# A late load, four sums in banks of their own, and a rewoven first period in a one-core attention and mixing kernel

## The chip, the cores and the metric

The kernel runs on one core of one Trainium2 chip. The metric is device time in microseconds (us) from start to end of one execution. The profile's span, from the first to the last instruction, is about 2 us shorter than the device time of the same execution.

## The reference

Two parts follow each other for a batch of B = 8. The first is a cross attention in both directions, for H = 8 heads, between S = 512 rows of x and 32 rows of a state, with head size 64:

```python
scores = scale * x @ state.T ;  a  = softmax(scores) ;  xread = a  @ state     # 512 rows
scores2 = scale * state @ x.T ; a2 = softmax(scores2) ; sread = a2 @ x         # 32 rows
attn = concat([xread, sread], rows)            # (8, 8, 544, 64), heads then side by side: (8, 544, 512)
```

The second is a mixing layer on these 544 x 512 values per batch:

```python
X = fft(fft(x, axis=1), axis=2) ; mixed = real(X)
u = x + mixed
un = (u - mean(u)) / sqrt(var(u) + 1e-6)
out = u + relu(un @ w_ch1) @ w_ch2             # w_ch1 512 x 2048, w_ch2 2048 x 512
```

The kernel does the transforms as products with cosine and sine tables: first over the 544 rows ("first axis"), then over the 512 columns ("second axis"). Rows are folded with their mirror images beforehand, so that half the tables are enough.

## The kernel before

Every engine runs its instructions in the order in which the program lists them, so the order of calls is the schedule. Batch 0 goes through an opening of its own; from then on, periods follow in which the two layers of batch b, the transform of batch b+1 and the attention of batch b+2 are interleaved. The change touches the opening and the first period. The names: `turn` transposes on TensorE, `score`, `read`, `sread` and `state_rows` are the attention of batch 0, `fold` adds rows to mirror images, `terms_of` and `out_of` are the first axis of batch 0 (four sums j = 0 to 3, kept in PSUM, then copied to G), `over_d` is the second axis, `turn_u` transposes the centred rows, `warm(n)` is n TensorE products without use that only keep the engine busy.

The loads of x at the start; batch 1 follows batch 0 at once:

```python
    def load_x(b):
        xs = wk.tile([128, 4 * dm], F32, name="xs", tag="xs")
        ...
        if b == 0:
            for queue, n in ((nc.sync, 3), (nc.scalar, 6), (nc.scalar, 7), (nc.scalar, 2), (nc.sync, None), (nc.sync, 4), (nc.sync, 5),
                             (nc.scalar, 0), (nc.sync, 1)):      # None: the state of batch 0; 6 and 7 are single rows
                ...
    load_x(0)
    load_state(1, 2)
    load_x(1)
    turn_in_dram(2, 3)
    load_state(2, 3, s_dram)
    ...
    for lo, k0, c, t in (...):                  # 4 x tensor_scalar, arguments of the second table
        nc.gpsimd.tensor_scalar(gi[:, lo:lo + 128], ...)
    ...
    cast_x(0, lo=2, hi=3)                       # GpSimd: x to bf16, a quarter at a time
    more_constants()
    clears(0)
    for i in (1, 0):
        cast_x(0, lo=i, hi=i + 1)
    load_w1(0, 2)                               # from the GpSimd queue
```

The opening and the first axis of batch 0. The sums 0 and 1 lie in one tile of two banks, the sums 2 and 3 in tiles of the second set of PSUM pools, which can be had only when the opening's pool is closed:

```python
        def begin():
            two_ = x2("gp")
            acc.update({0: two_[:, 0], 1: two_[:, 1], 2: qt("gp"), 3: qt("gp")})
            for j in range(4):
                nc.tensor.matmul(acc[j][:, 0:NM], ..., start=True, stop=False)
    ...
    warm(12); turn_state(); warm(6); turn_x0(3); warm(3); turn_x0(2); turn_ends(); warm(3)
    score(3); warm(4); score(2); warm(4); turn_x0(1); read(3)
    ...; low(); load_w1(2, 4); more_loads()     # more_loads: state of batch 1, clears, cast_x(1), load of w2
    warm(3); turn_x0(0); read(2); second_table(); warm(4); score(1); warm(4); score(0); warm(4)
    read(1); warm(4); read(0)
    sin_table(); sine_c(); sine_s(); sread(); warm(8); state_rows(); sine_low(); second_sines()
    opening.close()                             # then the pools psX, psQ, psF
    warm(8); begin(); warm(8)
    fold(1)
    ...                                         # NC, NS: negated tables, on VectorE
    terms_of(0, 1), terms_of(1, 1); terms_of(0, "low"), terms_of(1, "low")
    fold(0)
    terms_of(2, 1), terms_of(3, 1)
    terms_of(0, 0); out_of(0); terms_of(1, 0); out_of(1)
    terms_of(2, "low"), terms_of(2, 0); out_of(2)
    terms_of(3, "low"), terms_of(3, 0)
    second_halves()                             # VectorE, 2 instructions
    out_of(3)
    keep_low(); exp_again(); over_d(0)
```

(Several calls stand on one line here; in the program each has its own.) The first period before: a list in fixed order. Q(i, r) is a sixteenth of layer 1 of batch 0 (16 products of 128 x 128), s1 and r1 are the attention of batch 1, t1 is the transform of batch 1, M[...] are quarter steps of layer 2 of batch 0 (4 products of 128 x 512):

```python
    for step in (
            add_sums(0, 1), centre_sums(0, 1), over_d(1), add_sums(0, 0), centre_sums(0, 0),
            warm(8), turn_u(0, 1), Q(0, 0), turn_u(0, 0), ..., copies1[2], last_loads, Q(1, 2), s1[0], Q(0, 3), s1[1], Q(1, 3), s1[2], Q(2, 0), s1[3],
            r1[0], Q(2, 1), r1[2], r1[1], Q(2, 2), r1[3], Q(2, 3), r1[4], r1[5], low_state, load_x3, Q(3, 0), r1[7],
            state_ones(2, B), spread x 4, done, first_roots, Q(3, 1), Q(3, 2)):
        step()
    weave((Q(3, 3), 0, 0.25), (t1, 0.2, 1), ([M[i] for i in (0, 4, 1, 5, 2, 6, 3, 7, 8, 9)], 0.33, 0.99), ..., (scores_next, 0.46, 1))
```

`weave` gives each stream a stretch between 0 and 1, spreads its steps evenly over the stretch, and emits all steps in the order of their positions. r1[7] ends with `fold` of batch 1 on VectorE (13 instructions), and t1 begins with the four products of the first axis (`over_s`), which read what fold leaves.

Of the kernel before, what the change touches and what calls it, by code (L numbers as in the profile page):

```python
# [12 lines left out]
F32 = mybir.dt.float32  # L13
# [17 lines left out]
def kernel(  # L31
# [73 lines left out]
    def load_state(lo, hi, src=state):  # L105
        nc.sync.dma_start(
            out=stf[:, lo:hi].rearrange("p b g d -> p (b g) d"),
            in_=src[lo:hi].rearrange("b (g hh) j d -> (hh j) (b g) d", hh=4),
        )
# [2 lines left out]
    xs_of = {}  # L112

    def load_x(b):
        xs = wk.tile([128, 4 * dm], F32, name="xs", tag="xs")
        xs_of[b] = xs
        v = xs.rearrange("p (i h d) -> p i h d", i=4, d=D)
        xb = x[b].rearrange("h s d -> s h d")
        parts = [
            (slice(0, 128), 0, xb[1:129]),  # L120
            (slice(0, 128), 1, xb[144:272]),
            (slice(0, 128), 2, xb[273:401]),
            (slice(32, 128), 3, xb[416:512]),
            (slice(0, 15), 3, xb[129:144]),
            (slice(16, 31), 3, xb[401:416]),
            (slice(15, 16), 3, xb[0:1]),
            (slice(31, 32), 3, xb[272:273]),
        ]
        if b == 0:
            for queue, n in ((nc.sync, 3), (nc.scalar, 6), (nc.scalar, 7), (nc.scalar, 2), (nc.sync, None), (nc.sync, 4), (nc.sync, 5),  # L130
                             (nc.scalar, 0), (nc.sync, 1)):
                if n is None:
                    load_state(0, 1)
                    continue
                ps, si, rows = parts[n]
                queue.dma_start(out=v[ps, si], in_=rows)  # L136
            return
        for ps, si, rows in parts:
            nc.sync.dma_start(out=v[ps, si], in_=rows)

    def cast_x(b, copy=nc.gpsimd.tensor_copy, lo=0, hi=4):
        copy(xin_bufs[b % 2][:, lo:hi, 1:513], xs_of[b].rearrange("p (i c) -> p i c", i=4)[:, lo:hi])  # L142

    load_x(0)
    load_state(1, 2)
    load_x(1)


    def turn_in_dram(lo, hi):
        nc.sync.dma_start(out=s_dram[lo:hi].rearrange("b h j d -> (b h) j d"),  # L150
                          in_=state[lo:hi, :, ::-1, :].rearrange("b h j d -> (b h) j d"))

    turn_in_dram(2, 3)
    load_state(2, 3, s_dram)

    for i in range(2):
        nc.vector.memset(xin_bufs[i][:, :, 0:514:513], 1.0)
# [53 lines left out]
    def absolute(q, f):  # L211
        nc.vector.tensor_scalar(q.bitcast(I32), in0=f.bitcast(I32), scalar1=0x7fffffff, scalar2=None, op0=ALU.bitwise_and)


    def turn(W, N, lf, cols, scratch):
        n = len(cols)
        f2d, q2d = scratch[:, 0:n * W], scratch[:, n * W:2 * n * W]
        f, q = [t.rearrange("p (n w) -> p n w", w=W) for t in (f2d, q2d)]
        def ends():
            for i, c in enumerate(cols):  # L220
                nc.vector.scalar_tensor_tensor(f[:, i, :], in0=lf, scalar=pf[:, c:c + 1], in1=q[:, i, :], op0=ALU.mult, op1=ALU.add)
            absolute(q2d, f2d)

        for i, c in enumerate(cols):
            nc.vector.tensor_scalar(q[:, i, :], in0=lf, scalar1=pn[:, c:c + 1], scalar2=float(1 << 23), op0=ALU.mult, op1=ALU.add)
        nc.vector.tensor_scalar(q2d, in0=q2d, scalar1=float(1 << 23), scalar2=-float(N), op0=ALU.subtract, op1=ALU.mult)
        return f, q, ends

    shrink = 1.0 - 1e-6
# [10 lines left out]
    f1, q1, turn_ends = turn(NM, Stot, lt, [0, 2], gen1)  # L240

    gi = gen2[:, 0:512].bitcast(I32)
    for lo, k0, c, t in ((0, 0, 3, 128.0), (128, 128, 3, 128.0), (256, 0, 4, 256.0), (384, 128, 5, pf[:, 6:7])):
        nc.gpsimd.tensor_scalar(gi[:, lo:lo + 128], in0=li[:, k0:k0 + 128], scalar1=pf[:, c:c + 1], scalar2=t,
                                op0=ALU.mult, op1=ALU.add)

    def second_table():
        nc.vector.tensor_scalar(gi, in0=gi, scalar1=dm - 1, scalar2=None, op0=ALU.bitwise_and)
        nc.vector.tensor_scalar(sgi, in0=pi_[:, 3:4], scalar1=1, scalar2=None, op0=ALU.bitwise_and)
# [36 lines left out]


    cast_x(0, lo=2, hi=3)
    more_constants()
    clears(0)  # L290
    for i in (1, 0):
        cast_x(0, lo=i, hi=i + 1)

    def load_w1(lo, hi):
        for q in range(lo, hi):
# [2 lines left out]
    load_w1(0, 2)  # L298

    def more_loads():  # L300
        state_blocks(1, 2, nc.gpsimd.tensor_copy)
        clears(1)
        nc.gpsimd.memset(stb[:, 2:].rearrange("p b g c -> p (b g c)").bitcast(F32), 0.0)
        cast_x(1)
        for q in range(4):
            nc.gpsimd.dma_start(out=w2[:, q * 4:(q + 1) * 4, :], in_=w2v[:, q * 4:(q + 1) * 4, :])

# [8 lines left out]
    def x2(name):  # L316
        return psX.tile([128, 2, 512], F32, name=name, tag="x")
# [362 lines left out]
    def transform(b):  # L680
# [10 lines left out]
        acc = {}  # L691

        def begin():
            two_ = x2("gp")
            acc.update({0: two_[:, 0], 1: two_[:, 1], 2: qt("gp"), 3: qt("gp")})
            for j in range(4):
                nc.tensor.matmul(acc[j][:, 0:NM], lhsT=XN[:, 0, :], rhs=xin_bufs[0][:, 0, 0:NM], start=True, stop=False)

# [86 lines left out]
        def centre_sums(k, r):  # L785
            t = ub[k, r] = wk.tile([128, 512], BF16, name="ub", tag="ub", bufs=5)
            ud = U[k][:, r, 0:512] if r == 0 else U[k][:, 1, 512:0:-1]
            if (k, r) == (1, 0):
                nc.vector.tensor_scalar(t, in0=ud, scalar1=-512.0, scalar2=S_of[k, r][:, 0:1], op0=ALU.mult, op1=ALU.add)
            else:  # L790
                nc.scalar.activation(t, ud, AF.Identity, bias=S_of[k, r][:, 0:1], scale=-512.0)
# [197 lines left out]

    turn_state, turn_x0, score, read, sread, state_rows, fold, low = open_batch()  # L990
    begin, terms_of, out_of, keep_low, over_d, add_sums, centre_sums, turn_u, spread, done = transform(0)
    warm(12)
    turn_state()
    warm(6)
    turn_x0(3)
    warm(3)
    turn_x0(2)
    turn_ends()
    warm(3)
    score(3)  # L1000
    warm(4)
    score(2)
    warm(4)
    turn_x0(1)
    read(3)
    nc.vector.tensor_copy(XTs[0], XRs[0][0:32, 0, :])
    low()
    load_w1(2, 4)
    more_loads()
    warm(3)  # L1010
    turn_x0(0)
    read(2)
    second_table()
    warm(4)
    score(1)
    warm(4)
    score(0)
    warm(4)
    read(1)
    warm(4)  # L1020
    read(0)
    sin_table()
    sine_c()
    sine_s()
    sread()
    warm(8)
    state_rows()
    sine_low()
    second_sines()
    opening.close()  # L1030
    psX = ctx.enter_context(tc.tile_pool(name="psX", bufs=1, space=bass.MemoryType.PSUM))
    psQ = ctx.enter_context(tc.tile_pool(name="psQ", bufs=3, space=bass.MemoryType.PSUM))
    psF = ctx.enter_context(tc.tile_pool(name="psF", bufs=3, space=bass.MemoryType.PSUM))
    pool_of = {"warm": (psF, "c")}
    warm(8)
    begin()
    warm(8)
    fold(1)
    for t, n in ((TC, NC), (TS, NS)):
        nc.vector.tensor_scalar(n, in0=t[:, 0, :], scalar1=-1.0, scalar2=None, op0=ALU.mult)  # L1040
    terms_of(0, 1), terms_of(1, 1)
    terms_of(0, "low"), terms_of(1, "low")
    fold(0)
    terms_of(2, 1), terms_of(3, 1)
    terms_of(0, 0)
    out_of(0)
    terms_of(1, 0)
    out_of(1)
    terms_of(2, "low"), terms_of(2, 0)
    out_of(2)  # L1050
    terms_of(3, "low"), terms_of(3, 0)
    second_halves()
    out_of(3)
    keep_low()
    exp_again()
    over_d(0)
    pool_of.pop("tile")
    s1, reads_next = attend(1)
    load_x3 = lambda: (load_state(3, B, s_dram), load_x(3))
    scores_next, reads_after = attend(2)  # L1060
    L, M, r1, t1 = layer1(0), layer2(0), reads_next, transform(1)
    W = lambda n: (lambda: warm(n))
    turns1, copies1, s1 = s1[0], s1[1:4], s1[4:]
    Q = lambda i, r: L[4 * r + i]
    low_state = lambda: (state_blocks(2, 3, nc.gpsimd.tensor_copy), cast_x(2), turned[2]())
    for step in (
            lambda: add_sums(0, 1), lambda: centre_sums(0, 1), lambda: over_d(1), lambda: add_sums(0, 0), lambda: centre_sums(0, 0),
            W(8), lambda: turn_u(0, 1), Q(0, 0), lambda: turn_u(0, 0),
            lambda: (add_sums(1, 1), centre_sums(1, 1)), Q(1, 0), Q(0, 1),
            lambda: turn_u(1, 1), lambda: (add_sums(1, 0), centre_sums(1, 0)), Q(1, 1), Q(0, 2), turns1, lambda: turn_u(1, 0),  # L1070
            copies1[0], copies1[1], copies1[2], last_loads, Q(1, 2), s1[0], Q(0, 3), s1[1], Q(1, 3), s1[2], Q(2, 0), s1[3],
            r1[0], Q(2, 1), r1[2], r1[1], Q(2, 2), r1[3], Q(2, 3), r1[4], r1[5], low_state, load_x3, Q(3, 0), r1[7],
            lambda: state_ones(2, B), lambda: [spread(k, r) for k, r in ((0, 1), (0, 0), (1, 1), (1, 0))], done,
            lambda: [r() for r in first_roots], Q(3, 1), Q(3, 2)):
        step()
    L = L[:11] + [Q(3, 3)]
    weave((L[11:], 0, 0.25), (t1, 0.2, 1), ([M[i] for i in (0, 4, 1, 5, 2, 6, 3, 7, 8, 9)], 0.33, 0.99),
          ([lambda: state_blocks(3, B, nc.gpsimd.tensor_copy)], 0.85, 0.85), (scores_next, 0.46, 1))
    l2 = M
    for b in range(1, B + 1):  # L1080
        reads_next = reads_after
# [47 lines left out]
```

## Time and profile before

| what | value |
|---|---|
| device time, median of 3 | 312.06 us (312.06 to 312.41) |
| span of the profiled execution | 309.9 us |
| TensorE matmul busy | 290.8 us, 94% |
| TensorE weight loads busy | 166.6 us, 54% |
| VectorE, ScalarE, GpSimd busy | 179.4, 136.7, 94.2 us |
| first product of layer 1 of batch 0 | at 28.05 us |
| first product of layer 1 of batch 1 | at 69.37 us |

In the profile PE is TensorE, PEld its weight loads, DVE VectorE, ACT ScalarE, POOL GpSimd and SP the engine that issues most transfers; ACTq and SPq are the queues of instructions that only start transfers. A line of the timeline gives the start in us, the busy time in us, engine, source line, operation, output<-inputs, shapes and how often, and in brackets the idle time of the engine before it and what ended it. A line of the list of waits gives who waited for whom, the total in us, how often, and the longest. A line of the table by stretches gives the stretch, its length, the busy time of PE, PEld, DVE, ACT and POOL with the count of instructions, the granted TensorE clock (1 is full), the busy share of the 16 transfer engines (over 1 where transfers overlap) and GB/s.

### The profile page before, as it was taken

The page shows a single profiled execution, that of the slowest core. Times are in us where ns is not written, and L with a number is a line of the kernel's source. Part 1 is how long each engine was busy: PE and PEld are TensorE (multiplying, and loading weights), DVE is VectorE, ACT ScalarE, POOL GpSimd, SP SyncE. Part 2 cuts the span into 40 slices and gives each one's busy share as a digit, 9 for nine tenths or more (in the row PEclk, how much of TensorE's full clock was granted, in tenths as well). Part 3 has the DMA queues.
Part 4 walks back from the last instruction along what each step waited for, and adds up shares of the span by engine and source line. Part 5 has one row for each costly group of instructions (what it writes and reads, how often), then busy time and mean ns, then how long its engine had stood idle before and what let it go on. Part 6 is the DMA issues. An engine that isn't in the chain of part 4 may idle for free.

```text
span 309.9 us, 6001 instructions
## 1 busy us (share of the span) xinstructions
PE 290.8 (94%) x2289; PEld 166.6 (54%) x2320; DVE 179.4 (58%) x442; ACT 136.7 (44%) x257; POOL 94.2 (30%) x213
## 2 busy tenths in 40 slices
PE   3977995999999999999999999999999999999996
PEld 3956884544644555556645454445554544555443
DVE  5665359968697666871826846684859383100112
ACT  4656774374662445235451455235533533333300
POOL 7695047466046022800316013600340041000000
PEclk9999999899999999999999999999999999999999
DMA  7999950594763674268542495244243014500345
GB/s 155 189 194 188 196 114 17 105 176 105 172 103 84 143 166 117 59 130 154 136 103 77 86 186 128 72 92 115 68 104 68 34 53 102 102 36 34 70 123 148
DMA packets 110906, 34.86 MB, mean 113 GB/s; under 512 B 102062, under 2 KB 106414, under 8 KB 110878
## 3 DMA queue, kind: packets, MB, share of 16 engines
q1 hardware_dynamic: 100126, 28.72, 43.6%
q0 software_dynamic: 4224, 4.19, 8.4%
q10 hardware_dynamic: 6528, 1.58, 2.3%
q8 instruction: 18, 0.29, 0.4%
q14 instruction: 10, 0.08, 0.1%
HBM read 22.41 MB, written 14.02 MB: 118 GB/s over the span
## 4 chain that ended last, share of the span: by engine, by line
PE 84%; DVE 7%; ACT 4%; issue 2%; ACTq 1%; POOL 0%; DVEq 0%
PE po L956 35%; PE ph L892 33%; PE gp L755 3%; PE ph L902 2%; PE warm L988 1%; PE yp L662 1%; PE po L948 1%; PE xrp L441 1%; PE xfp L441 1%; PE yp L661 1%; ACTq L136 1%; PE esp L416 1%; DVE U L666 1%; PE eTp L428 1%; PE srp L480 1%
## 5 line engine op out<-in xcount | busy, mean ns | idle before, releaser
L956 PE MATMUL po<-w,hT 128*128 128x512 bf16 x478 | 122.8, 382 | 1.6 <-issue 0.9
L894 ACT ACTIVATE hT<-ph 128x512 bf16<-128x512 f32 x112 | 66.8, 598 | 118.4 <-PE ph L892 116.3
L892 PE MATMUL ph<-unT,w 128*128 128x512 bf16 x435 | 112.7, 379 | 0.7
L892 PEld LDWEIGHTS <-w 128*128 128x128 bf16 x576 | 50.6, 98 | 47.4 <-issue 0.6
L956 PEld LDWEIGHTS <-hT 128*128 128x128 bf16 x496 | 47.3, 99 | 47.1 <-issue 1.1
L923 DVE SCALAR_TENSOR_TENSOR ot<-po,rstd,U 128x512 f32<-128x512 f32 (+2 forms) x33 | 24.2, 733 | 51.4 <-PE po L956 49.2
L759 POOL COPY GL<-G 128x128 bf16<-128x128 bf16 x7 | 2.0, 290 | 72.7 <-ACT G L756 72.7
L666 DVE TENSOR_TENSOR U<-yp,XR 128x512 f32<-128x512 f32 x14 | 9.6, 683 | 22.2 <-PE yp L662 22.2
L327 POOL TENSOR_TENSOR rstd<-mv,epst 128x1 f32<-128x1 f32 x34 | 7.2, 212 | 49.0 <-DVE mv L323 49.0
L321 DVE BATCH_NORM_STATS2 st<-U 128x6 f32<-128x512 f32 x32 | 21.7, 679 | 0.0
L328 POOL TENSOR_TENSOR rstd<-rstd,mhalf 128x1 f32<-128x1 f32 x34 | 20.0, 587 | 2.7
L756 ACT CAST G<-gp 128x288 bf16<-128x288 f32 x28 | 13.3, 485 | 10.8 <-PE gp L755 10.8
L902 PE MATMUL ph<-unT,w 128*128 128x128 bf16 x256 | 16.4, 219 | 0.9 <-ACT unT L822 0.9
L142 POOL CAST xin<-xs 128x2048 bf16<-128x2048 f32 (+1 forms) x10 | 15.5, 1555 | 2.3 <-DMA xs<-in_x_dram 2.2
L902 PEld LDWEIGHTS <-w 128*128 128x128 bf16 x256 | 15.0, 98 | 1.2 <-issue 1.0
L492 POOL COPY XT<-XR 32x514 bf16<-32x514 bf16 x7 | 4.2, 603 | 36.2 <-DVE XR L450 36.1
L988 PE MATMUL warm<-ident 128*128 128x128 bf16 x83 | 9.1, 258 | 4.2 <-POOL ident masks.py:199 3.5
L810 DVE TENSOR_SCALAR ub<-U,mv 128x512 bf16<-128x512 f32 x24 | 12.3, 511 | 0.9
L904 ACT ACTIVATE hT<-ph 128x512 bf16<-128x512 f32 x16 | 9.2, 596 | 3.3 <-PE ph L902 3.2
L450 DVE TENSOR_TENSOR XR<-xrp,rs 128x512 bf16<-128x512 f32 x14 | 9.7, 695 | 0.6
L450 DVE TENSOR_TENSOR XF<-xfp,rs 128x512 bf16<-128x512 f32 x14 | 9.7, 692 | 0.5
L666 DVE TENSOR_TENSOR U<-yp,XF 128x510 f32<-128x510 f32 x14 | 9.5, 677 | 0.0
(226 smaller groups left out, 375.8 us busy)
## 6 DMA issues: line engine op xcount, KB each, us to landing
xs<-in_x_dram SPq DMA_DIRECT2D x22, 256.0 KB, 5.4
w<-in_moe_w_ch_dram POOLq DMA_DIRECT2D x8, 512.0 KB, 8.6
out_dram<-ot SPq DMA_DIRECT2D x15, 256.0 KB, 3.8
r_dram<-ot SPq DMA_DIRECT2D x14, 256.0 KB
out_dram<-r_dram SPq DMA_DIRECT2D x14, 256.0 KB, 3.5
xs<-in_x_dram SPq DMA_DIRECT2D x8, 192.0 KB, 4.3
xs<-in_x_dram ACTq DMA_DIRECT2D x2, 256.0 KB
l_dram<-ot SPq DMA_DIRECT2D x2, 256.0 KB
```

The lines of the kernel that those rows point to most:

```text
L142: copy(xin_bufs[b % 2][:, lo:hi, 1:513], xs_of[b].rearrange("p (i c) -> p i c", i=4)[:, lo:hi])
L321: nc.vector.bn_stats(st6, u)
L328: nc.gpsimd.tensor_tensor(rstd, rstd, mhalf, op=ALU.pow)
L450: nc.vector.tensor_tensor(ov, in0=p[ps, :, 0:256].rearrange("p g (h d) -> p g h d", d=D), in1=rs[ps].unsqueeze(3).to_broadcast([n, 2, 4, D ...
L666: nc.vector.tensor_add(u.rearrange("p (k r) -> p k r", r=2), p.rearrange("p (r k) -> p k r", r=2)[:, 0:u.shape[1] // 2, :], x.rearrange("p ...
L756: nc.scalar.copy(G[:, j, :].rearrange("p (i q) -> p q i", q=2), p[:, 0:NM].rearrange("p (q i) -> p q i", q=2))
L810: nc.vector.tensor_scalar(t, in0=ud, scalar1=mv[:, 0:1], scalar2=None, op0=ALU.subtract)
L892: nc.tensor.matmul(ph[:, o:o + n], lhsT=w1[:, c, f * 128:(f + 1) * 128], rhs=un_of[key][:, c, :], start=(c == 0), stop=(c == DC - 1))
L894: nc.scalar.activation(hT[:, per * i:per * i + per, :].rearrange("p a b -> p (a b)"), ph, AF.Relu, scale=-1.0 / 512 if key == 0 else -1.0 ...
L902: nc.tensor.matmul(ph[:, o:o + 128], lhsT=w1[:, c, f * 128:(f + 1) * 128], rhs=un_of[key][:, c, 128 * r:128 * r + 128], start=(c == 0), st ...
L923: nc.vector.scalar_tensor_tensor(ot[:, cols], in0=po_of[i][:, 0:cols.stop - cols.start], scalar=rstd, in1=u[:, cols], op0=ALU.mult, op1=AL ...
L956: nc.tensor.matmul(po_of[i], lhsT=h_of[key][:, f, i * 128:(i + 1) * 128], rhs=w2[:, f, :], start=(f == 0), stop=(f == FC - 1))
```

## The change

It has three parts. The load of batch 1 no longer starts right after that of batch 0: a GpSimd memset into its buffer, placed behind the casts of batch 0, holds it back, and the loads of batch 0 are fewer and in another order. The four sums of the first axis get a bank each in the opening's own PSUM pool, so that they can be begun before the pool is closed. And the first period is woven by position, with layer 2 of batch 0 following layer 1 as filler for the transform of batch 1. Smaller moves go with it: other numbers of warm products, the table arithmetic on VectorE and GpSimd earlier or later, one centring on VectorE instead of ScalarE.

```diff
     def load_x(b):
+        row = v[15:32:16, 3]
...
-            (slice(15, 16), 3, xb[0:1]),
-            (slice(31, 32), 3, xb[272:273]),
+            (row, xb[0:273:272]),
...
-            for queue, n in ((nc.sync, 3), (nc.scalar, 6), (nc.scalar, 7), (nc.scalar, 2), (nc.sync, None), (nc.sync, 4), (nc.sync, 5),
-                             (nc.scalar, 0), (nc.sync, 1)):
+            for queue, n in ((nc.sync, None), (nc.scalar, 2), (nc.sync, 3), (nc.scalar, 0), (nc.sync, 4), (nc.sync, 5), (nc.sync, 6),
+                             (nc.sync, 1)):
...
     load_x(0)
-    load_state(1, 2)
-    load_x(1)
+    xs_of[1] = wk.tile([128, 4 * dm], F32, name="xs", tag="xs")
...
     cast_x(0, lo=2, hi=3)
+    for lo, k0, c, t in (...):                 # the 4 tensor_scalar, moved here
     more_constants()
-    clears(0)
     for i in (1, 0):
         cast_x(0, lo=i, hi=i + 1)
+    nc.gpsimd.memset(xs_of[1][0:1, 0:1], 0.0)
+    load_state(1, 2)
+    load_x(1)
+    turn_in_dram(2, 3)
+    load_state(2, 3, s_dram)
+    clears(0)
...
         def begin():
-            two_ = x2("gp")
-            acc.update({0: two_[:, 0], 1: two_[:, 1], 2: qt("gp"), 3: qt("gp")})
+            for j, tag in enumerate("ttee"):
+                acc[j] = ps0.tile([128, 512], F32, name="gp", tag=tag, bufs=2)
...
-            if (k, r) == (1, 0):               # centring on VectorE
+            if (k, r) in ((0, 0), (1, 0)):
...
+    warm(22); turn_state(); warm(8); turn_x0(3); turn_x0(2); turn_ends(); second_table(); warm(3)
+    score(3); score(2); read(3); turn_x0(1); ...; low(); load_w1(2, 4); state_blocks(1, 2)
+    read(2); turn_x0(0); warm(2); score(1); warm(2); score(0); warm(3); read(1); warm(3); read(0)
+    sin_table(); sine_c(); sine_s(); sread(); begin(); warm(10); state_rows(); sine_low(); second_sines(); warm(14)
+    fold(1); ...; terms_of(0, 1), terms_of(1, 1); terms_of(0, "low"), terms_of(1, "low"); fold(0)
+    second_halves(); more_loads()              # more_loads begins with cast_x(1)
+    terms_of(2, 1), terms_of(3, 1); terms_of(2, "low"), terms_of(3, "low")
+    terms_of(0, 0); out_of(0); terms_of(1, 0); out_of(1); terms_of(2, 0); out_of(2); terms_of(3, 0); out_of(3)
+    warm(8); opening.close()                   # then the pools psX, psQ, psF
+    over_d(0); exp_again(); add_sums(0, 1); centre_sums(0, 1); over_d(1); warm(12); turn_u(0, 1); add_sums(0, 0); centre_sums(0, 0)
+    Q(0, 0); last_loads(); turn_u(0, 0); ...; Q(1, 0); Q(0, 1); ...; Q(1, 1); turns1(); turn_u(1, 0); Q(0, 2); copies1
+    Ls = the other eleven Q, in the order (1,2) (0,3) (1,3) (2,0) (2,1) (2,2) (2,3) (3,0) (3,1) (3,2) (3,3)
+    weave((Ls + [M[i] for i in (0, 4, 1, 5, 2, 6, 3, 7, 8, 9)], 0, 1), (s1, 0.03, 0.18), (r1, 0.18, 0.45), (t1, 0.52, 0.95),
+          ([state_ones(2, B), spread x 4, first_roots, done], 0.44, 0.6), ([later_state], 0.5, 0.5), ([load_x3], 0.9, 0.9),
+          ([state_blocks(3, B)], 0.96, 0.96), (scores_next, 0.75, 1))
```

The lines with + from `warm(22)` on are abridged: several calls stand on one line.

## The prediction

> **What bounds the kernel now.** I read first the table by stretches, cut where the timeline shows stages to begin and end: ident ready, last scores, first term of the first axis, first product of layer 1, the r1[7] products, end of the fold, end of the slow clock, first layer 1 product of batch 1, end.
>
> ```profile
> core 0: us, PE busy (x) PEld busy (x) DVE busy (x) ACT busy (x) POOL busy (x), PEclk, DMA share, GB/s
> 12.00:19.70 7.70, 6.11 (x124) 5.34 (x123) 7.00 (x30) 6.71 (x11) 6.21 (x14) 1.00 1.13 173
> 19.70:28.05 8.35, 5.72 (x55) 3.68 (x53) 4.04 (x15) 4.20 (x8) 7.47 (x13) 1.00 1.14 195
> 28.05:46.10 18.05, 17.14 (x286) 16.20 (x286) 8.05 (x24) 12.41 (x25) 2.84 (x5) 1.00 0.97 163
> 46.10:53.00 6.90, 3.50 (x54) 3.11 (x54) 6.23 (x10) 3.55 (x7) 6.39 (x10) 1.00 0.04 10
> 53.00:58.60 5.60, 5.37 (x29) 3.19 (x31) 5.14 (x21) 1.45 (x3) 1.95 (x6) 0.70 0.40 78
> 69.40:309.90 240.50, 235.50 (x1596) 122.97 (x1621) 134.78 (x299) 95.70 (x180) 53.80 (x112) 1.00 0.46 102
> ```
>
> From 69.4 us on TensorE is busy 98% of the time (235.5 of 240.5), and the change doesn't touch that code: the gain must come before 69.4. There TensorE idles 2.6 us at 19.7 to 28.05 and 3.4 us at 46.1 to 53; at 53 to 58.6 it is busy, but at a granted clock of 0.70. Before 19.7 its busy time says little, as much of it is `warm`. So I went on to the timeline of the first 60 us, for what each stage waits for:
>
> ```profile
> 0.73 3.10 ACTq L136 DMA_DIRECT2D xs<-in_x_dram  x4
> 3.86 1.28 ACT L177 ACT_TABLE_LOAD   x1 [3.86 <-issue]
> 5.26 1.21 ACT L166 CAST stb<-gen 32x128 bf16<-32x128 f32 x4
> 9.08 1.60 POOL L142 CAST xin<-xs 128x512 bf16<-128x512 f32 x2 [1.18 <-DMA xs<-in_x_dram]
> ...
> 18.36 0.61 PE L988 MATMUL warm<-ident 128*128 128x128 bf16 x8 [0.73 <-ACT XR L634]
> ...
> 24.31 0.27 PE L661 MATMUL yp<-TEO,G 128*128 128x256 bf16 x1 [0.33 <-DVE TEO L271]
> ```
>
> ScalarE issues four loads until 3.83 and can only then load its table and cast the state, on which the first transposes wait. GpSimd waits 1.18 us for x of batch 0, while batch 1's load has been issuing since 4.70. At 18.36 the new pools wait for a copy out of the old one. At 24.31 the second axis waits for its table. Last, TensorE's waits from 20 to 80 us:
>
> ```profile
> PE gp L755 <- DVE XQ L517: 1.8, 1, 1.8
> PE gp L755 <- DVE XQ L518: 1.6, 1, 1.6
> PE ph L902 <- ACT unT L822: 0.9, 1, 0.9
> PE tp L819 <- ACT ub L791: 0.7, 1, 0.7
> PE gp L708 <- ACT G L738: 0.6, 1, 0.6
> ```
>
> The two longest are the fold of batch 1 on VectorE; the last is a term waiting for a copy of the other half of its tile.
>
> **What the Trainium skill says.** "TensorE: Matmul & The Clock Gate", Part 1: the array runs at half rate until it has been busy for a window of about 3.4 us, and goes back after an idle one. The trace agrees: a 128-column product starts every 0.11 us until about 12 us and every 0.055 after, and after the fold's two waits (1.8 and 1.6 us) the 512-column products take 0.43 us each instead of 0.22, until about 57 us. "DMA: Bandwidth & Descriptors", Queues, rings and completion order: each engine takes turns between the queues that have work. The trace fits: from 4.6 to 14 us both x batches move together at 205 GB/s. "SBUF — State Buffer", Who interferes with whom: a VectorE instruction with two SBUF inputs and a GpSimd one that reads SBUF exclude each other. In the fold the same addition takes 0.55 us (L517) and 2.11 us (L518), the second beside a GpSimd cast from 50.71 to 52.68.
>
> **Part 1, the opening.** ScalarE issues two loads instead of four. Its first took 1.27 us, a later one about 0.6 (from the chain of waits), so it is free at about 2.5 instead of 3.83, has its table at 3.8 and casts the state from 3.9 to 5.1 (before 5.26 to 6.47). TensorE is then bound by the 22 warm products: 3.46 + 22 x 0.11 = 5.8, against 6.53 for the last transposes of the state. Then come 8 warm ones (0.9), two transposes (0.43 each), 3 warm (0.3), one score (0.64), a second; the warm products between the scores are gone. That puts the first `read` at about 9.6, against 11.5; busy without a break from 3.46, TensorE may also reach full clock some microseconds before 12. The casts of batch 0's other rows follow GpSimd's 1.6 us of table arithmetic and 0.7 us of constants: at about 7.1 to 8.7 instead of 9.08 to 10.68, as their data no longer shares the engines. From there ScalarE sets the pace, with four exponentials and two copies of 0.6 us, and then the sine table, at about 12.8 instead of 14.78. VectorE's four reads (0.9 each) end at about 14.4 instead of 16.77. The heads' product, the tables and fold(1) follow, so the first term could come 2.0 earlier. A further 1.3 comes from `begin`, now before the heads' product: after it there is no pool to wait for (0.73), and 14 warm products stand there (about 0.8) instead of 1.9 us of warm, begin, warm at 18.36 to 19.7. Together 3.3: the first term at 16.4 instead of 19.7. Every step of this assumes data in time, and the order of loads is new (a quarter of x needs four transfers of one queue). I count 2.3.
>
> **Part 2, terms to layer 1** (19.7 to 28.05 before). One bank per sum: the 0.6 wait of L708 goes, and 0.2 to 0.3 of issue gaps with it. The second table's halves (0.85 + 0.53 on VectorE) come before the last terms rather than after: the last copy to G doesn't wait for them; it ran at 24.44, 0.46 after the last term. 0.5. The centring of (0,0) leaves ScalarE (0.72, at 27.02), so the copy of unT follows the transposes directly: 27.2 instead of 27.65. 0.45. The exponential's table load stays on ScalarE beside VectorE's add. Sum 1.75; I count 1.6. Layer 1 would begin 3.9 earlier, at about 24.1. w1's first half is issued at about the same time as before (10.6) and landed after 7.3 us in the median, so it is there.
>
> **Part 3, the first period.** Before r1[7] now stand 14 Q instead of 13, after it two instead of three. From r1[7] to the fold's first result pass 4.85 us (46.10 to 50.95), and two Q fill about 2: TensorE idles 2.4 to 2.7 there, 0.5 to 0.9 more than before. Against this, the second wait (1.6) gets M[0] (0.86) as filler. And with less idle in one stretch the clock may not fall: between 53 and 58.6 the 0.70 costs 5.6 x 0.3 = 1.7 us. I give it six chances in ten: 1.0. So -0.5, +0.9, +1.0: 1.4 gained. Something is given back: the bn_stats of batch 0 (four, 0.85 with aggregation, 3.4 us) stand on VectorE between the fold and the first add of batch 1, as before, so the chain fold, statistics, add, centre, transpose goes earlier only as the fold does, by about 3.4; only two M and a score of batch 2 lie between over_d(0) and the transpose that needs 3 us of VectorE and ScalarE. When TensorE is ahead by more, it waits there. 0.9 back.
>
> **Part 4, what the late load costs.** The transfer engines stand empty from about 7.5 to 9.6, some 2 us. They were full from 14 to 43 us, so the last x of batch 2 lands at about 45 instead of 43. Its cast was at 50.71 before; if all else is 4 us earlier, it is wanted at about 46. The w2 load lands before it; layer 2 wants it from about 47. Nothing lost, but nearly.
>
> **Sum:** 2.3 + 1.6 + 1.4 - 0.9 = 4.4 us. 312.06 - 4.4 = 307.6.
>
> **Rivals.** (a) The gain of the opening is eaten by data: the casts of batch 1 come after 22 us, w2 goes out later, and TensorE, 4 us earlier, waits for w2 or batch 2's x. For it: 29 us of full transfer engines and the hole in Part 4. Against it: SP's next load already waited for the cast of batch 1 at 24.1, and this cast comes no later if batch 1 lands by 20. It would leave 310 to 312. (b) The fold stays the bound of the first period: a longer single wait at the first over_s, the clock falls as before, and the new weave gains nothing, or loses 1 to 2 us behind the statistics. For it: one Q less behind r1[7]. Then 308.5 to 310. (c) All goes as worked out without discounts (opening 3.3, terms 1.75, clock kept 1.7 and M 0.9, no more than 0.5 back): a gain of about 6.5, 305.5. For it: every wait that the change goes for is there in the trace; against it: four serial chains (loads, ScalarE, GpSimd, VectorE) must all move by the same amount.
>
> **Range and chances.** Case (c) with some luck gives the lower end, 304.8; (a) the upper, 311.2. 2% is 6.2 us, below 305.8, which needs nearly all of (c): 0.20. Slower by 2% would need 6 us lost in 70: 0.03. Within 2%: 0.77.
>
> **What would show it right or wrong.** The table load of ScalarE at 2.5 instead of 3.86; the casts of batch 0 done by 9; the first term (L708 before) at 16.4 to 17.5; no wait of a term for a copy to G; the first Q near 24; one fold wait of 2.4 to 2.7 and a second under 1; granted clock 1.0 after it; the first layer 1 product of batch 1 near 65. The prediction is wrong if the casts of batch 0 still wait for data, if TensorE waits for w1, w2 or xin of batch 1 or 2, if the clock after the fold still falls, or if the time after 69.4 changes by over 0.5 us.

## The result, and the profile after

The change made the kernel slower: 321.37 us (319.74 to 322.82) against 312.06, a ratio of 1.029 with a 95% interval of 1.024 to 1.034. The prediction was 307.6 us with a range to 311.2.

The profiled execution has a span of 319.5 us. First the table by stretches of the kernel after, cut at the same events as before: first term of the first axis, first product of layer 1, the r1[7] products, the fold's first product, first product of the second axis of batch 1, and then the stretch round the start of layer 1 of batch 1 and the rest.

```profile
core 0: us, PE busy (x) PEld busy (x) DVE busy (x) ACT busy (x) POOL busy (x), PEclk, DMA share, GB/s
17.06:24.32 7.26, 6.02 (x64) 4.41 (x64) 5.07 (x21) 4.36 (x9) 1.27 (x4) 1.00 1.22 200
24.32:48.41 24.09, 19.66 (x303) 18.76 (x303) 8.04 (x24) 12.81 (x26) 10.62 (x17) 0.93 0.98 168
48.41:54.74 6.33, 2.17 (x37) 1.97 (x35) 5.67 (x9) 1.82 (x4) 5.60 (x9) 0.83 0.16 32
54.74:61.60 6.86, 6.86 (x35) 3.71 (x36) 5.58 (x22) 2.55 (x5) 2.81 (x8) 0.66 0.50 83
74.50:89.50 15.00, 11.96 (x94) 5.58 (x93) 8.72 (x22) 4.58 (x9) 8.28 (x13) 0.89 0.67 122
89.50:319.50 230.00, 226.98 (x1537) 117.78 (x1533) 126.00 (x278) 90.98 (x173) 48.50 (x102) 1.00 0.47 102
```

The opening did what it was meant to do: layer 1 begins at 24.32 instead of 28.05. In the next row TensorE idles 4.4 us (24.09 less 19.66) where before it idled 0.9, then 4.2 us round the fold (before 3.4), then it is busy at a clock of 0.66 (before 0.70), and near 80 us it idles 3.0 us more. The waits of TensorE from 20 to 100 us name them (who waited for whom, total us, how often, longest):

```profile
PE gp L756 <- DVE XQ L518: 4.2, 1, 4.2
PE ph L893 <- ACT hT L895: 3.0, 1, 3.0
PE xTp L389 <- POOL xin L141: 2.9, 1, 2.9
PE eTp L406 <- ACT xT L395: 1.2, 1, 1.2
PE xrp L442 <- ACT ET L430: 1.1, 1, 1.1
```

The distance between the two kernels, taken at five events of both timelines (us), shows where each part of the loss falls:

| event | before | after | after less before | change since the row above |
|---|---|---|---|---|
| first product of layer 1, batch 0 | 28.05 | 24.32 | -3.7 | -3.7 |
| r1[7], last read of batch 1's attention | 46.10 | 48.41 | +2.3 | +6.0 |
| first product after the fold of batch 1 | 50.98 | 54.74 | +3.8 | +1.5 |
| first product of layer 1, batch 1 | 69.37 | 74.52 | +5.2 | +1.4 |
| product of layer 1 behind the first scores after it | 79.64 | 89.53 | +9.9 | +4.7 |

From the last row to the end both need the same: 309.9 - 79.64 = 230.3 and 319.5 - 89.53 = 230.0 us. So 13.6 us are lost between 24 and 90 us, and nothing behind. The timeline of the kernel after gives the story of each loss (start, busy us, engine, line, operation, output<-inputs, and in brackets the idle time and its releaser):

```profile
9.43 9.95 SPq L138 DMA_DIRECT2D xs<-in_x_dram  x7
9.86 1.72 POOL L298 DMA_DIRECT2D w<-in_moe_w_ch_dram  x2
15.41 1.54 POOL L298 DMA_DIRECT2D w<-in_moe_w_ch_dram  x2
29.77 2.00 POOL L141 CAST xin<-xs 128x2048 bf16<-128x2048 f32 x1 [11.31 <-DMA xs<-in_x_dram]
31.82 1.69 PE L389 MATMUL xTp<-ident,xin 128*128 128x128 bf16 x16 [2.90 <-POOL xin L141]
...
51.93 2.27 POOL L141 CAST xin<-xs 128x2048 bf16<-128x2048 f32 x1
52.36 1.86 DVE L517 COPY XE<-SS 128x2 f32<-128x2 f32 x1
54.74 0.30 PE L756 MATMUL gp<-TC,XQ 128*128 128x144 bf16 x1 [4.17 <-DVE XQ L518]
...
68.35 0.37 SPq L938 DMA_DIRECT2D r_dram<-ot  x1
72.35 0.42 SPq L106 DMA_DIRECT2D gen<-s_dram  x1
76.46 2.98 POOL L161 CAST stb<-gen 32x640 bf16<-32x640 f32 x4 [6.36 <-DMA gen<-s_dram]
79.48 1.09 ACT L895 ACTIVATE hT<-ph 128x512 bf16<-128x512 f32 x2 [6.57 <-POOL stb L161]
80.13 1.86 PE L893 MATMUL ph<-unT,w 128*128 128x512 bf16 x4 [3.04 <-ACT hT L895]
```

The instructions of the same loads, casts and copy in the kernel before:

```profile
4.70 8.46 SPq L139 DMA_DIRECT2D xs<-in_x_dram  x8
10.62 1.72 POOL L296 DMA_DIRECT2D w<-in_moe_w_ch_dram  x2
22.22 1.89 POOL L142 CAST xin<-xs 128x2048 bf16<-128x2048 f32 x1
...
50.09 0.26 DVE L516 COPY XE<-SS 128x2 f32<-128x2 f32 x1
59.49 0.59 SPq L106 DMA_DIRECT2D gen<-s_dram  x1
```

Three groups. **x of batch 1:** its held load is issued from 9.43 on, but 0.4 us later the load of w1 starts beside it, and GpSimd waits 11.3 us for the data; TensorE's transposes stand behind its cast. **The fold:** a copy of two elements per partition takes 1.86 us on VectorE instead of 0.26, and ends when GpSimd's cast of batch 2 does (54.22 and 54.20). **Batch 3:** its load now stands in SP's queue behind the first stores (68.35) and is issued at 72.35, instead of 59.49 before. The cast of its state waits 6.4 us for it at the head of GpSimd's queue, ScalarE then waits for GpSimd and TensorE for ScalarE.

### The profile page after: what moved, and what is told of

The parts are those of the page before. It is cut to its first block, busy times and chain, and to the rows that moved or that the text cites. A ratio compares the mean times of both kernels' runs of the same rounds, so it can differ in the third digit from the quotient of the medians.

```text
span 319.5 us, 6034 instructions
## 1 busy us (share of the span) xinstructions
PE 296.2 (93%) x2324; PEld 168.0 (53%) x2324; DVE 179.7 (56%) x443; ACT 135.6 (42%) x256; POOL 94.8 (30%) x214
## 4 chain that ended last, share of the span: by engine, by line
PE 79%; DMA 7%; DVE 5%; POOL 4%; ACT 1%; SPq 1%; issue 1%; POOLq 0%; DVEq 0%
PE po L957 35%; PE ph L893 32%; DMA xs<-in_x_dram 5%; PE gp L756 3%; PE ph L903 2%; DMA gen<-s_dram 1%; POOL xin L141 1%; PE po L949 1%; PE yp L663 1%; PE yp L662 1%; PE xrp L442 1%; POOL stb L161 1%; PE esp L417 1%; DVE U L667 1%; SPq L138 1%
## 5 line engine op out<-in xcount | busy, mean ns | idle before, releaser
L957 PE MATMUL po<-w,hT 128*128 128x512 bf16 x496 | 126.9, 385 | 0.0
L893 PE MATMUL ph<-unT,w 128*128 128x512 bf16 x448 | 114.7, 381 | 3.0 <-ACT hT L895 3.0
L893 PEld LDWEIGHTS <-w 128*128 128x128 bf16 x576 | 50.8, 98 | 50.6 <-issue 4.0
L141 POOL CAST xin<-xs 128x2048 bf16<-128x2048 f32 (+1 forms) x10 | 15.8, 1587 | 12.4 <-DMA xs<-in_x_dram 11.3
L903 PEld LDWEIGHTS <-w 128*128 128x128 bf16 x256 | 15.7, 101 | 1.3 <-issue 1.1
L989 PE MATMUL warm<-ident 128*128 128x128 bf16 x87 | 8.2, 252 | 3.5 <-POOL ident masks.py:199 3.5
L488 DVE TENSOR_TENSOR XR<-srp,rcs 32x128 bf16<-32x128 f32 x24 | 6.9, 287 | 5.9 <-POOL XT L493 4.4
## 6 DMA issues: line engine op xcount, KB each, us to landing
w<-in_moe_w_ch_dram POOLq DMA_DIRECT2D x8, 512.0 KB, 10.9
```

The lines of the kernel that those rows point to most:

```text
L893: nc.tensor.matmul(ph[:, o:o + n], lhsT=w1[:, c, f * 128:(f + 1) * 128], rhs=un_of[key][:, c, :], start=(c == 0), stop=(c == DC - 1))
L903: nc.tensor.matmul(ph[:, o:o + 128], lhsT=w1[:, c, f * 128:(f + 1) * 128], rhs=un_of[key][:, c, 128 * r:128 * r + 128], start=(c == 0), st ...
L957: nc.tensor.matmul(po_of[i], lhsT=h_of[key][:, f, i * 128:(i + 1) * 128], rhs=w2[:, f, :], start=(f == 0), stop=(f == FC - 1))
```

## The experiments

Theory A says that two separate waits for data cost the most: x of batch 1 is late because w1 is loaded beside it (about 4.5 us), and batch 3's load is late in the weave (about 4.7 us). Theory B says that these are one cause, the late batch 1. Theory C takes the weave itself, with too little filler at the fold, for the loss. Theory L came up on the way: GpSimd's casts keep VectorE out. (The expectation of e6 calls this "the lock".) Every kernel ran beside the kernel before, whose median there was 312.0 to 312.3 us; ratios are to those runs.

**e1: the load of batch 1 no longer held** (the rest of the change as it is).

```diff
     load_x(0)
-    xs_of[1] = wk.tile(...)
+    load_state(1, 2); load_x(1); turn_in_dram(2, 3); load_state(2, 3, s_dram)
...
-    nc.gpsimd.memset(xs_of[1][0:1, 0:1], 0.0)
-    load_state(1, 2); load_x(1); turn_in_dram(2, 3); load_state(2, 3, s_dram)
```

> The changed kernel with the load of batch 1 issued right behind that of batch 0, as before; all else as changed. Theory A (two separate data waits: batch 1's x lands late because it shares the transfer engines with w1, cost about 4.5 us; batch 3's load stands late in the weave, cost about 4.7 us): the wait for x of batch 1 at 29.77 goes, the cast of batch 1 ends before 24, the late load of batch 3 stays; 316 to 317.5 us. Theory B (one cause: everything after follows from the late batch 1): 311 to 312.5. Theory C (the new weave with its fold gap is the loss, data waits only fill the gap): over 319.

Measured: 320.86 us, 1.027 (1.022 to 1.033). Only C's number fits (over 319), and not for C's reason. The wait for x of batch 1 is gone, but nothing is gained: layer 1 begins at 28.09 instead of 24.32. The timeline of e1 shows why:

```profile
19.47 1.89 POOL L141 CAST xin<-xs 128x2048 bf16<-128x2048 f32 x1
19.49 3.94 DVE L270 TENSOR_SCALAR TEO<-TEO,sg 128x512 bf16<-128x512 bf16 x1
24.58 0.27 PE L662 MATMUL yp<-TEO,G 128*128 128x256 bf16 x1 [2.66 <-DVE G L739]
```

With the data early, GpSimd's cast and five memsets behind it fill 19.47 to 23.3 us. The second table's half, 0.34 us on VectorE in the kernel after, lasts 3.94 us beside them, and the second axis waits 2.7 us for the copy to G that comes after; the clock is 0.66 from 25 to 30 us. A wait of 2.9 us was traded for one of 2.7. This led to theory L.

**e2: batch 3's load earlier in the weave; e3: e1 and e2 together.**

```diff
-([load_x3], 0.9, 0.9)
+([load_x3], 0.5, 0.5)
```

> The changed kernel with the load of batch 3 moved from position 0.9 to 0.5 of the first period, behind the cast and transposes of batch 2; all else as changed. Theory A: its issue moves from 72.4 to about 61, GpSimd's wait of 6.4 us for the state goes, and with it TensorE's 3.0 us and the slow clock behind it; 316 to 317.5 us. Theory B: the load is late only because batch 1 was; it stays a wait; 320 to 321.5. Theory C: no more than 1 us gained.

> Both edits, batch 1's load early and batch 3's load at 0.5. Theory A: the gains add, 310.5 to 312.5 us, because the wait at the fold (4.2 us) and the slow clock after it are left. Theory B: like the first edit alone. Theory C: over 316.

Measured: e2 316.32 us, 1.011 (1.008 to 1.014); e3 315.91 us, 1.011 (1.006 to 1.016). e2 is as A expected: the load is issued at 60.96, the wait of 3.0 us near 80 is gone, and 5.1 us come back although batch 1 is as late as before. So B falls: batch 3 is a loss of its own. e3 fits none of the three (A expected 310.5 to 312.5): that the early load of batch 1 adds nothing agrees with e1. Three of e2's 15 runs, the profiled one among them, were in a slower state; without them its median is 316.1, which moves each difference taken with it below by 0.2.

**e4: w1 behind the held load of batch 1** (both halves of w1 where its second half was); **e5: e4 and e2 together.**

```diff
     cast_x(0, lo=i, hi=i + 1)
-    load_w1(0, 2)
...
     low()
-    load_w1(2, 4)
+    load_w1(0, 4)
```

> The changed kernel with batch 1's load held as it is, but the first half of w1 issued with the second (about 15 us instead of 9.9), so that batch 1's x has the transfer engines alone until then. Theory A (the sharing with w1 made it late, not the hold alone): batch 1's cast begins before 22 instead of 29.77, the first layer 1 products may wait for w1 by up to 2 us; 316.5 to 319 us. Rival (the hold and the slow issue of the load make it late whatever else moves): the cast begins after 26, and the time stays at 320 or more.

> The changed kernel with the first half of w1 issued with the second, and the load of batch 3 at 0.5. Theory A (two separate data waits, each now removed by an edit that worked alone: about 5 us each): 310 to 312 us. Rival (one wait takes the place of the other, as when the early load of batch 1 gained nothing): 314 to 316.

Measured: e4 315.61 us (315.13 to 319.18), 1.014 (1.007 to 1.021), better than expected; e5 311.17 us, 0.998 (0.996 to 1.000), as A expected. The timeline of e4:

```profile
9.61 5.07 SPq L138 DMA_DIRECT2D xs<-in_x_dram  x7
15.48 3.20 POOL L298 DMA_DIRECT2D w<-in_moe_w_ch_dram  x4
20.08 1.89 POOL L141 CAST xin<-xs 128x2048 bf16<-128x2048 f32 x1
```

With w1 out of the way the same seven transfers take 5.07 us to issue instead of 9.95, and batch 1 is cast at 20.08 instead of 29.77, without any other change: w1's bytes made it late. The two gains add, 5.8 and 4.4 us (e4's four runs scatter by 4 us, so tenths don't count here).

The fold's longest wait fell too, from 4.2 to 2.5 us, which was not expected. The timeline of e5 at the fold:

```profile
48.48 0.16 DVE L515 COPY XE<-SS 128x2 f32<-128x2 f32 x1
48.68 0.43 DVE L516 TENSOR_TENSOR XQ<-XE 128x256 bf16<-128x256 f32 x1
49.00 2.19 POOL L141 CAST xin<-xs 128x2048 bf16<-128x2048 f32 x1 [1.01 <-DMA xs<-in_x_dram]
49.35 1.86 DVE L518 CAST XN<-XE 128x2 bf16<-128x2 f32 x1
```

(The fold's lines have numbers lower by two here: the copy is L515.) The copy that took 1.86 us takes 0.16 here. Batch 2's load is being issued until 47.44 us here (38.32 in the kernel after), GpSimd waits 1.01 us for it, and its cast then meets a VectorE instruction *behind* the fold's first result instead of one ahead of it.

**e6: e5 with batch 2's casts on ScalarE.**

```diff
-    later_state = lambda: (state_blocks(2, 3, nc.gpsimd.tensor_copy), cast_x(2), turned[2]())
+    later_state = lambda: (state_blocks(2, 3), cast_x(2, nc.scalar.copy), turned[2]())
```

> The same, with the state and the x of batch 2 cast by ScalarE instead of GpSimd. Theory L (GpSimd's casts keep VectorE out while it folds: a 2-element copy took 1.86 us beside the cast): no fold instruction above 0.9 us, TensorE's fold waits together 1.5 us shorter or more, the time 1 to 2.5 us lower than without this edit. Rival (the fold's own chain and the two Q behind it make the wait, the lock is hidden): within 0.7 us of it, or slower as ScalarE delays its copies.

Measured: 310.22 us, 0.994 (0.993 to 0.996), 0.95 less than e5, just under what L expected. No VectorE instruction of the fold takes over 0.8 us any more, and in the profiled execution the clock stays at 1.00 from 40 to 60 us (e5: 0.76 from 50 to 55). That execution, at 309.1 us, is one of 7 in 20 whose mean clock was 0.999 or more; e5 has 7 such too. The medians of these differ by 1.8 us, those of the other 13 by 0.8, so the gain isn't the clock's alone. L holds for the VectorE instructions, but its 1.5 us at TensorE's fold waits didn't come: the first wait is 2.4 us after 2.5, the fold's own length behind r1[7].

**e7: e3 with GpSimd's cast of batch 1 held** until the second table is made, by a one-element copy that reads it.

```diff
     def more_loads():
+        nc.gpsimd.tensor_copy(gate[:, 3:4], TEO[:, 3, 1, 127:128])
         cast_x(1)
```

> Batch 1's load early and batch 3's load at 0.5, as in the third run, and in addition GpSimd's burst of casts, clears and memsets held until VectorE has done the second table's halves (by a one-element copy that reads them). Theory L (this burst kept VectorE out: the half took 3.94 us against 0.35, and the second axis waited 2.7): the half takes under 0.5 us, TensorE's wait of 2.7 goes, 311 to 313 us. Rival (VectorE is late there for another reason): no change, 315 to 316.

Measured: 312.91 us, 1.002 (1.000 to 1.004), as L expected. The table's half takes 0.34 us, the wait of 2.7 us is gone, and 3.0 us with it. This is e1's loss made and unmade by GpSimd's place alone.

**e8: new opening and sums, w1 behind batch 1, but the first period in the old order; e12: the same with w1 at its place**, so the change with its weave left out.

```diff
-    Ls = ...; weave((Ls + [M[i] ...], 0, 1), (s1, 0.03, 0.18), (r1, 0.18, 0.45), (t1, 0.52, 0.95), ...)
+    for step in (keep_low, Q(0, 0), turn_u(0, 0), ...): step()      # the list of the kernel before from there on
+    weave((Q(3, 3), 0, 0.25), (t1, 0.2, 1), ([M[i] ...], 0.33, 0.99), ..., (scores_next, 0.46, 1))
```

> The new opening and sums with w1 behind batch 1's x, and the first period in the order of the kernel before (batch 3's load is early in it). Theory A with the weave as a loss of its own: it has three Q behind the fold's products and the opening is 3.5 us earlier, so 308 to 309.5 us, below the fifth run. Rival (the weave is worth something once its loads are in time): 311 or more, above the fifth run.

> The changed kernel with its opening and sums as they are (load of batch 1 held, w1 at its place), but the first period in the old order: the weave is left out. It is the kernel with the old period and w1 behind the load of batch 1, at 308.4 us, with w1 moved back. Theory A (the shared engines cost the same whatever the period): 3.5 to 5.5 us more, 312 to 314, with the cast of batch 1 waiting until about 29.8 us, TensorE waiting 2 to 4 us for it near 30 to 34 us, and the x of batch 2 cast 4 us later or more than at 48.8. Rival: the old period takes the late batch 1 better, as its transposes come later and its other work fills the wait: less than 2 us more, under 310.4.

Measured: e8 308.37 us, 0.989 (0.985 to 0.993), as expected. e12 310.45 us, 0.995 (0.993 to 0.996): faster than before, and 2.1 us above e8, where A expected 3.5 to 5.5 and the rival under 2. So A's size for the late batch 1 holds only inside the weave; C, that the weave itself costs, has a large share. The waits of e12:

```profile
PE gp L756 <- DVE XQ L518: 1.8, 1, 1.8
PE gp L756 <- DVE XQ L519: 1.6, 1, 1.6
PE xTp L389 <- POOL xin L141: 1.5, 1, 1.5
```

Batch 1 is cast at 29.70, as late as in the kernel after, but the wait for it is 1.5 us instead of 2.9 (the clock falls behind it here too, to 0.53 from 34 to 36 us). The waits of 1.2 and 1.1 us in batch 1's attention are not there, and the fold has the two waits of the kernel before. e8 has a new wait instead (a line of its waits: the scores of batch 2 for a transpose of x):

```profile
PE esp L415 <- DMA xT<-xin: 2.6, 2, 1.7
```

**e9: e8 with the scores of batch 2 later in the weave.**

```diff
-(scores_next, 0.46, 1))
+(scores_next, 0.66, 1))
```

> The eighth run (new opening, w1 behind batch 1's x, old order of the first period) with the scores of batch 2 spread over 0.66 to 1 instead of 0.46 to 1. If its wait of 2.6 us for the transposed x of batch 2, with the slow clock after it, is what is left of the late load there, 2 to 3 us less than the eighth run: 305.5 to 306.8. Rival (VectorE's statistics of batch 0, between fold and add, hold that stretch anyway): within 1 us of it.

Measured: 307.74 us (306.61 to 310.05), 0.987 (0.983 to 0.991). That wait is gone, but only 0.6 us of median came of it, and the intervals of e8 and e9 overlap. Three of e9's six runs took 306.6 to 306.8 us, less than any of e8's, and three 308.7 to 310.1; what separates them is not shown. It has the lowest median of the study, and is faster than both kernels.

**e10: the kernel before with the sums in banks of their own**, begun before the heads' product, with the order of terms and the earlier table halves that go with it; no hold, no weave.

```diff
-            two_ = x2("gp")
-            acc.update({0: two_[:, 0], 1: two_[:, 1], 2: qt("gp"), 3: qt("gp")})
+            for j, tag in enumerate("ttee"):
+                acc[j] = ps0.tile([128, 512], F32, name="gp", tag=tag, bufs=2)
```

> The kernel before with only the sums changed: a bank each in the opening's pool, begun before the heads' product, the second table's halves earlier, the terms in the new order; loads, first period and centring as before. By the prediction's part 2 and the pool wait of part 1: 2 to 2.8 us less than before, 309.3 to 310. Rival, theory L (moved earlier, the halves meet GpSimd's burst of casts and clears and are blocked, as in the first run): no more than 1 us gained, and a half of over 2 us on VectorE.

Measured: 309.11 us, 0.990 (0.988 to 0.992), 3.1 us less than the 312.19 beside it. Layer 1 begins at 25.57 us. This part alone has most of what the change can gain: with the new opening too, e8 begins layer 1 at 24.31 and is only 0.7 below in time, and the intervals overlap.

**e11: e9 with the hold behind the first cast only**, at about 5.5 us, w1 at its old place and GpSimd's later casts held as in e7.

> The ninth run with batch 1's load held only behind the first cast of batch 0 (about 5.5 us instead of 9.6), the first half of w1 back at its place, and GpSimd's burst held behind the table's halves. If the hole in the transfers is what makes batch 2's x late, it lands about 3 us earlier and the time is equal or up to 1 us lower than the ninth run. Rival (w1 and batch 0's last rows share with it again): 1 us or more above the ninth run.

Measured: 309.71 us, 0.992 (0.989 to 0.995), 2.0 above e9, the size that the rival named, though the intervals just overlap. Its reason isn't what the profile shows: batch 1 is cast at 20.60 without a wait for data. The first term is 1.0 us later than in e9 (17.99 for 16.96), where the eight transposes at 8.3 us took 1.04 us instead of 0.62. And batch 2 lands in time now, but that puts GpSimd's cast on the fold again: waits of 1.8 and 1.6 us, and a clock of 0.50 from 50 to 55 us (e9: 1.00). Three of the six runs have the mean clock of the profiled one, 0.988; the other three took 308.5 to 308.8 us.

## Why the prediction was wrong

The medians (us) of six kernels with the new opening and sums separate the causes. The 95% intervals reach 0.4 us (e12) to 2.2 us (e4) to each side, so the differences taken from them are good to 1 or 2 us:

| | first period in the old order | woven, load of batch 3 at 0.5 | woven, load of batch 3 at 0.9 |
|---|---|---|---|
| w1 at its place | 310.45 (e12) | 316.32 (e2) | 321.37 (after) |
| w1 behind the load of batch 1 | 308.37 (e8) | 311.17 (e5) | 315.61 (e4) |

**Right: Parts 1 and 2.** ScalarE starts its table load at 1.90 us, GpSimd's casts of batch 0 end at 9.05, the first term is at 17.06 (predicted 16.4 to 17.5), no term waits for a copy to G, and layer 1 begins at 24.32 (predicted 24.1). That it is so close is in part luck, as two errors partly cancel: the first term came 2.6 us earlier instead of the counted 2.3, and the stretch from there to layer 1 shrank by 1.1 (8.35 to 7.26) instead of 1.6. In it, 0.67 us pass from the last term's end to the second axis, 0.33 before: Part 2's 0.5 for the table halves didn't come. (Part 1's "1.9 us of warm, begin, warm" adds busy times that overlap; the stretch lasts 1.34, and its 1.3 follows from that.) ScalarE's first cast of batch 0 still waits 2.6 us for its data, with the first term in its range all the same. e8 keeps the gain of both parts to the end, 3.6 us; e10, with the banks but not the new opening, 3.1.

**Failed: Part 4, "Nothing lost, but nearly".** It counted the hole in the transfers (they did move nothing from 7.5 to 9.5 us) but not what the held load meets. "This cast comes no later if batch 1 lands by 20", said rival (a): it was cast at 29.77, because w1 was issued 0.4 us behind it, as e4 shows; Part 2 had left w1 at "about the same time as before". Before, batch 1's load was issued from 4.70 to 13.16 us, most of it ahead of w1's first half at 10.6. "DMA: Bandwidth & Descriptors", Queues, rings and completion order, has the rule that was cited and not applied here: engines take turns between queues. The trace fits it: a transfer of this load took 12.6 to 16.8 us from issue to landing beside w1, and 4.9 to 6.1 in e4. By the first column this costs 2.1 us, in the weave 5.2 (e2 less e5).

**Failed: Part 3, "1.4 gained" and "0.9 back", and nothing for the load of batch 3.** The weave did not gain 0.5 us but lost 10.9 (after less e12). 5.1 of them is the load of batch 3 at 0.9 (after less e2), which the diff shows and the prediction didn't work out: behind the stores in SP's queue, with a GpSimd cast next at 0.96. Of the other 5.9, 2.8 stay when batch 1 is in time (e5 less e8); 3.1 come only with both. Against e12 the timeline of the kernel after places them: r1[7] at 48.41 instead of 46.48, though its layer 1 begins 0.4 earlier (2.3 us, where the wait for batch 1 and those of 1.2 and 1.1 us stand); from there to the fold's first product 6.33 instead of 4.89 us (1.4); from there to layer 1 of batch 1 19.8 instead of 18.1 (1.7, with the clock at 0.66). What share the dense attention of batch 1 (0.03 to 0.45) has in the first of these was not tried alone.

**Mis-sized: the fold.** Rival (b) had the mechanism, a longer single wait after which the clock falls. The wait was put at 2.4 to 2.7 us; that is what e5 and e6 show (2.5 and 2.4), but in the kernel after a two-element copy of 1.86 us brought it to 4.2. "SBUF — State Buffer", Who interferes with whom, says that copies can take the ports shared with GpSimd, and that the second to come is blocked until the other ends. The trace agrees: the copy begins at 52.36 and ends at 54.22, with the cast that runs from 51.93 to 54.20. The prediction knew this lock from L518 and placed it behind the first result, where it stood before.

**The sum.** Up to the first Q the prediction was off by 0.2 us (3.7 for 3.9). Behind it stood 0.5 us of gain, and 13.6 were lost in the profile. Of the signs of being wrong, TensorE's wait for x of batch 1 and the falling clock after the fold came true, and so did "the time after 69.4 changes": from the first layer 1 product of batch 1 to the end it takes 245.0 us instead of 240.5. This one was the most useful: it pointed at batch 3, and at the claim that "the change doesn't touch that code", which fell with the move of that load.

## What to carry to other kernels

Holding a load back left room only where nothing else was issued into the gap (e4 against the kernel after); look at what starts in the same microsecond, and put the bytes that are wanted first ahead of it. In a rewoven schedule, check for every load what stands before it in its issuing queue (stores wait for results) and what stands behind its consumer in that engine's order. Earlier data isn't always better: it moves a GpSimd cast as well, and this one cost nothing only where it missed VectorE's chain.

## What the runs showed of the hardware

- A VectorE tensor_scalar of 128x512 bf16 took 0.34 us alone and 3.94 beside a GpSimd cast of 1.89 us with five memsets right behind it (e1): it ended after the last memset (23.43 and 23.29 us), not after the cast. With the series held back it took 0.34 again (e7). Copies and casts of 128x2 on VectorE took 0.16 and 0.17 us alone (e6) and 1.86 beside a GpSimd cast (the kernel after, e5).
- The granted clock fell from 1.00 to 0.50 for 3.4 us or twice that, at times that lie on a grid: in the kernel after it changes at 32.08, 35.49, 52.56, 59.38 and 79.86 us, which are 1, 5, 2 and 6 steps of 3.41 us apart. How busy TensorE was in the step before went with each fall: 0.51 and 1.43 us before those at 32.08 and 52.56, 0.66 in the kernel before (53.25), 1.12 in e5 (48.98), 1.53 in e12 (34.12). In the two steps of e12 that hold the fold's waits (47.77 to 54.59) it was busy 1.79 and 1.61 us, and the clock stayed at 1.00. So the same two waits, of 1.8 and 1.6 us, brought it down in the kernel before and not in e12, and a single one of 2.5 us did in e5 where 2.4 did not in e6. Executions of one kernel differ too: of 20 of e6, 7 have a mean clock of 0.999 or more and 13 of 0.994 or less. "TensorE: Matmul & The Clock Gate", Part 1, says that the window of about 3.4 us runs freely; the grid agrees. It names an idle window for the fall; in these traces one in which TensorE was busy for less than half was enough.
- The same seven transfers of batch 1 took 9.95 us to issue beside w1 (the kernel after) and 5.07 without it (e4).
